# Linear attention with a gated MLP on one core: attention's last product in native fp32 with tokens on partitions, x normalized and turned before it leaves the chip, the fill finishing h with tanh, and blocks of 512 columns

## The chip, the core and the metric

The kernel runs on one core of a Trainium2 chip. Its engines work side by side and wait for each other by semaphores: TensorE (PE in the profile; PEld are its weight loads), VectorE (DVE), ScalarE (ACT), GpSimd (POOL), and SyncE (SP), which issues most DMAs. The metric is device time in microseconds from the first to the last instruction, lower is better.

## The reference, cut to what matters

```
phi(x):  proj = x @ w_phi;  proj -= max|proj|;  [exp(proj), exp(-proj)]      # 64 -> 2 x 128 features
kv  = phi(k)^T @ v          z = sum_s phi(k)                                  # per head
out = phi(q) @ kv / (phi(q) . z + 1e-6)                                       # B=8, H=8, S=576, D=64
x   = out, heads side by side: 4608 tokens x 512
xn  = x / sqrt(mean(x^2) + 1e-6) * rms_g
h   = silu(xn @ w_gate) * (xn @ w_val)                                        # 512 -> 1536, twice
result = h @ w_out                                                            # 1536 -> 512
```

All arrays are fp32.

## The kernel before, in words

Full precision is reached in two ways. A tile can be split into a rounded high part and a rest (`_split`, L59 to L61: a cast on ScalarE and a subtraction on VectorE or GpSimd), both in the type fp32r, and a product then takes three matmuls (high x high, high x low, low x high). Or a matmul takes fp32 operands as they are, which is called native fp32 below.

The work has three stages, all of it in one order that a scheduler of the framework makes from the program as written.

**Attention, with the first part of the MLP filled in.** 32 pairs of heads (8 batches x 4) run in a pipeline, one step of the loop at L500 per pair: `front` of pair i (transposes L298, projection in three fp32r matmuls L311 to L313, maximum L315, subtraction L318), `mid` of pair i-1, `back` of pair i-2, `last` of pair i-3. `mid` takes the exponentials of k (L338), makes kv with z as a 65th column in native fp32 (L351: 16 products of 128x128 with 128x65 per pair, two more with the remainder of 64 tokens, L346), splits kv into high and low (`kvs_`, L356), turns y of q so that features lie on partitions (L364), takes its exponential twice, in fp32 and rounded (L375, L376), and lets GpSimd subtract the two for the low half (L380). `back` multiplies with features as the contraction and kv as the stationary operand, 288 tokens at a time: 24 matmuls per pair (L415), evicted by ScalarE (L417) with the denominator in row 64. The denominator goes through DRAM to be spread over partitions, is inverted (L425), goes through DRAM again to be broadcast (L428), and `last` scales (L442, L443) and stores x by features (xs). A block of 288 columns that is complete in DRAM is fetched (`load_x`), split (`fill`, L465), and multiplied by the first three of the twelve column blocks of w_gate and w_val (`unit`, L474: 12 matmuls each); the products go to DRAM (gvs). rms_g has been multiplied into those weights.

Beside it the weights are decoded piece by piece (`decode_pieces`): one piece per step of the loop here, 24 pieces of w_out in the second stage.

**Gate and value.** 12 blocks of 384 columns, each with nine column blocks j: `gv` does 24 matmuls (L588) and silu times value (`hidden`, L571, L573), and h goes to DRAM (hs). `prep` (L145) fetches the next block of x, sums squares with a matmul against ones, normalizes and splits. `gv_raw` fetches the raw products of the fill, scales them with 1/rms and finishes them. The gate and value weights are loaded during the first block (`load_gv`, L561). The loop at L633 also pops the pieces of w_out, three a block from the second block on, and, once none are left, calls `load_o` (L608) at its steps 2 and 6 until four weight blocks of the output product are ready. `load_o` takes four DMAs into one of two buffers named wc, makes four differences in the other (L615) and splits both into wh and wl; its tiles lie in a pool of their own for the first four calls and in a pool that follows the gate and value weights in memory for the last two (L720).

**Output.** 18 groups of 256 tokens. `omm` (L737) does the seven products of Strassen's scheme, 18 matmuls of 256 columns each over the six weight blocks (L742); `operands` prepares the sums and splits of the next group.

Of the kernel before, what the change touches and what calls it, by code (L numbers as in the profile page):

```python
# [17 lines left out]

# [64 lines left out]
def kernel(ctx: ExitStack, tc: tile.TileContext, q, k, v, w_phi,  # L83
# [11 lines left out]
    SH = S // 2  # L95
    assert D == 64 and F == 128 and SR == 64 and T0 == 4 and NP == NC
    J1 = 3
    T = 384
    NB = N // T
    TF = S // 2  # L100
# [6 lines left out]
    gvs = dram.tile([J1 * 2 * 128, N], F32, name="gvs")  # L107
# [3 lines left out]
    wos = dram.tile([DF, DM], F32, name="wos")  # L111

    gl = ctx.enter_context(tc.tile_pool(name="gl", bufs=1))
    eps = gl.tile([128, 1], F32, name="eps")
    nc.vector.memset(eps, 1e-6)
    g = gl.tile([128, NC], F32, name="g")


# [4 lines left out]
    xm = x_ctx.enter_context(tc.tile_pool(name="xm", bufs=1))  # L123
    xops = [x_ctx.enter_context(tc.tile_pool(name="xo0", bufs=1))]
    xips = [x_ctx.enter_context(tc.tile_pool(name="xip", bufs=1))]
    xsv = xs.rearrange("(c p) n -> p c n", p=128)
    gvv = gvs.rearrange("(j w p) n -> j p w n", w=2, p=128)
    hsv = hs.rearrange("(j p) n -> p j n", p=128)

    one = gl.tile([128, 1], F32, name="one")  # L130
    nc.vector.memset(one, 1.0)
    epsd = gl.tile([128, 1], F32, name="epsd")
    nc.vector.memset(epsd, 0.0)
    nc.vector.memset(epsd[64:65], 1e-6)
    warm = gl.tile([128, 1], F32, name="warm")
    nc.scalar.activation(warm, one, AF.Exp)
    ones = gl.tile([128, 128], F32R, name="ones")
    nc.vector.tensor_copy(ones, one.broadcast_to([128, 128]))

    def fetch(bk, n=T, queue=None):  # L140
        x = xips[-1 if bk % 2 else 0].tile([128, NC * T], F32, name="x")[:, 0:NC * n].rearrange("p (c t) -> p c t", c=NC)
        (queue or nc.sync).dma_start(out=x, in_=xsv[:, :, bk * n:(bk + 1) * n])
        return x

    def prep(bk, x, pool, name):  # L145
        ss = xm.tile([128, T], F32, name="ss", bufs=1)
        nc.scalar.activation(ss, x[:, 0], AF.Square)
        for c in range(1, NC):
            sq = xm.tile([128, T], F32, name="sq", bufs=1)
            nc.scalar.activation(sq, x[:, c], AF.Square)  # L150
            nc.gpsimd.tensor_tensor(ss, ss, sq, ALU.add)  # L151
        sp = pool.tile([128, T], F32, name=name)
        sh = xm.tile([128, T], F32R, name="sq", bufs=1)
        sl = xm.tile([128, T], F32R, name="fo", bufs=3)
        _split(nc, sh, sl, ss, lo_eng=nc.gpsimd)
        nc.tensor.matmul(sp[:, 0:T], ones, sh, start=True, stop=False)
        nc.tensor.matmul(sp[:, 0:T], ones, sl, start=False, stop=True)
        ri = xm.tile([128, T], F32, name="ri", bufs=2)
        nc.scalar.activation(ri, sp[:, 0:T], AF.Sqrt, scale=1.0 / DM, bias=eps)
        nc.vector.reciprocal(ri, ri)  # L160
        for c in range(NC):
            nc.vector.scalar_tensor_tensor(x[:, c], x[:, c], g[:, c:c + 1], ri, ALU.mult, ALU.mult)
        xhl = xops[bk % len(xops)].tile([128, 2, NC, T], F32R, name="xb")
        _split(nc, xhl[:, 0], xhl[:, 1], x, lo_eng=nc.gpsimd)
        return xhl[:, 0], xhl[:, 1], ri
# [21 lines left out]

    a_ctx = ExitStack()
    xfp = a_ctx.enter_context(tc.tile_pool(name="a_xf", bufs=2))
    xips.append(a_ctx.enter_context(tc.tile_pool(name="a_xi", bufs=1)))  # L190
# [4 lines left out]
    big = a_ctx.enter_context(tc.tile_pool(name="a_big", bufs=2))  # L195
    dsc = a_ctx.enter_context(tc.tile_pool(name="a_dsc", bufs=3, space=DRAM))
# [6 lines left out]

# [9 lines left out]

    vms = [const.tile([128, 2, T0, D + 1], F32, name=f"vm{i}") for i in range(3)]
    vrs = [const.tile([128, 2, D + 1], F32, name=f"vr{i}") for i in range(3)]
# [5 lines left out]

    kvs = [[const.tile([128, 2, 2, 128], F32R, name=f"kv{i}{n}") for n in "hl"] for i in range(2)]
    for kp in kvs:
        for x in kp:
            nc.vector.tensor_copy(x[:, :, :, 64:128], w2[:, 2, 0:64].unsqueeze(1).unsqueeze(1).broadcast_to([128, 2, 2, 64]))

    def decode_jobs():
        jobs, late_ = [], []  # L230
        n = J1 * 128
        for wi, src in enumerate((w_gate, w_val)):
            for c in range(NC):
                def fill_w(w, wi=wi, c=c):
                    nc.vector.tensor_scalar(w, w, g[:, c:c + 1], None, ALU.mult)
                    _split(nc, wf1[wi][0][:, c], wf1[wi][1][:, c], w)
                jobs.append((src[c * 128:(c + 1) * 128, 0:n], n, fill_w))
# [29 lines left out]
    def load(pr):  # L267
# [14 lines left out]
        st[pr] = dict(kt=kt, qt=qt, rb=rb, hp=hp, b=b, vm=vm, vr=vr, kv=kvs[pr % 2])  # L282

    def front(pr):
# [7 lines left out]
        def trans(n):  # L294
            m = len(us[n]) * 128
            tp = ps_s.tile([128, 512], F32, name="sm")
            for j, u in enumerate(us[n]):
                nc.tensor.transpose(out=tp[:, j * 128:(j + 1) * 128], in_=u, identity=ident)  # L298
# [26 lines left out]
    def mid(pr):  # L325
        d = st[pr]
        y, vm, vr, (kh, kl) = d["y"], d["vm"], d["vr"], d["kv"]
        acc = ps_k.tile([128, 2, 2, D + 1], F32, name="acc")
        qh = big.tile([128, 2, 2, S], F32R, name="qh")
        ql = big.tile([128, 2, 2, S], F32R, name="ql")  # L330
        d.update(qh=qh, ql=ql)
# [12 lines left out]

# [9 lines left out]
        def kvs_():  # L354
            av = acc.rearrange("p a h d -> p h a d")
            _split(nc, kh[:, :, :, 0:D + 1], kl[:, :, :, 0:D + 1], av)  # L356


        def qexp(n, h):
            m = 4 if n == "q" else 1  # L360
            yp = ps_s.tile([128, 512], F32, name="sm")
            for j in range(m):
                src = y[n, h][:, j] if n == "q" else y[n, h][:, 1]
                nc.tensor.transpose(out=yp[:, j * 128:(j + 1) * 128], in_=src, identity=ident)  # L364
            if n == "q":
                hi, lo = qh[:, :, h, 0:SM], ql[:, :, h, 0:SM]
                eq = wk.tile([128, 2, 512], F32, name="eq")
                ei, yi = eq, yp
            else:
                hi, lo = qh[:, :, :, SM:S], ql[:, :, :, SM:S]  # L370
                eq = wk.tile([128, 2, 128], F32, name="eqr", bufs=1)
                ei = eq.rearrange("p a (h s) -> p a h s", h=2)
                yi = yp[:, 0:128].rearrange("p (h s) -> p h s", h=2)
            for sg in range(2):
                nc.scalar.activation(ei[:, sg], yi, AF.Exp, scale=1.0 - 2.0 * sg)  # L375
                nc.scalar.activation(hi[:, sg], yi, AF.Exp, scale=1.0 - 2.0 * sg)  # L376
                if n == "q":
                    for c in range(0, SM, SM // 2):
                        cs = slice(c, c + SM // 2)
                        nc.gpsimd.tensor_tensor(lo[:, sg, cs], ei[:, sg, cs], hi[:, sg, cs].bitcast(F32), ALU.subtract)  # L380
            if n != "q":
                nc.gpsimd.tensor_tensor(lo, ei, hi.bitcast(F32), ALU.subtract)
# [4 lines left out]
            lambda: qexp("q", 0),  # L387
# [3 lines left out]
            lambda: qexp("r", 0),  # L391
            lambda: qexp("q", 1),
# [3 lines left out]
            kvs_,  # L396
        ]


    def back(pr):  # L400
        d = st[pr]
        (kh, kl), qh, ql = d["kv"], d["qh"], d["ql"]
        nd = [big.tile([128, S], F32, name="nd", bufs=4) for _ in range(2)]
        dr = big.tile([128, S // 64], F32, name="dr", bufs=3)
        dd = dsc.tile([2, S], F32, name="dd")
        di = dsc.tile([2, S], F32, name="di")

        def num(h, c):
            cs = slice(c * SH, (c + 1) * SH)

            o = ps_f.tile([128, T], F32, name="fp") if pr < 12 else ps_s.tile([128, 512], F32, name="sm")
            i = 0
            for sg in range(2):
                for a, e in ((kh, qh), (kh, ql), (kl, qh)):
                    nc.tensor.matmul(o[:, 0:SH], a[:, h, sg], e[:, sg, h, cs], start=(i == 0), stop=(i == 5))  # L415
                    i += 1
            nc.scalar.activation(nd[h][0:D + 1, cs], o[0:D + 1, 0:SH], AF.Identity, bias=epsd[0:D + 1])  # L417
            if c == 1:
                nc.sync.dma_start(out=dd[h:h + 1], in_=nd[h][D:D + 1])
# [80 lines left out]
    for i in range(PR + 3):  # L500
# [18 lines left out]
        if len(units) <= 3:  # L519
            landed()  # L520
# [285 lines left out]
```

## Time and profile before

| | us |
|---|---|
| median of three runs | 1333.33 (1332.76 to 1334.62) |
| span of the profiled execution | 1337.6 |
| TensorE busy in it | 1288.5 |
| VectorE, ScalarE, GpSimd busy | 885.0, 711.0, 605.5 |
| first gate and value matmul (L588) starts | about 542 |
| first output matmul (L742) starts | about 1066 |

The profiled execution has no time of its own beside its span; the span lies 4.3 us above the median of the three runs. In the lines of the profile, `out<-in` are the program's tile names, `xN` the number of instructions, then come busy time, mean duration in ns, and the idle time before them with what ended it. Matmuls overlap, so the rate of TensorE is read from the distance of their starts. A native fp32 product has two records in the trace.

### The profile page before, as it was taken

The numbers are of one execution on the slowest core, as the hardware profiler recorded it, in microseconds if no ns is written. First come the engines' busy times: TensorE is split into PE (matmuls) and PEld (weight loads), VectorE is DVE, ScalarE is ACT, GpSimd is POOL, SyncE is SP. The second block draws the span as 40 slices with busy tenths as digits, with TensorE's granted clock in tenths as the row PEclk, the third lists the DMA queues.
The fourth block names the chain that finished last, engine by engine and source line by source line (L and its number), as shares of the span: only waits on it lengthen the run. The fifth ranks groups of instructions, "written<-read, shape, count | busy, mean of one in ns | idle before, by whom it ended". The sixth has DMA issues, their size and how long they took to land.

```text
span 1337.6 us, 25479 instructions
## 1 busy us (share of the span) xinstructions
PE 1288.5 (96%) x9396; PEld 1275.6 (95%) x9396; DVE 885.0 (66%) x1301; ACT 711.0 (53%) x1510; POOL 605.5 (45%) x568
## 2 busy tenths in 40 slices
PE   7989999999999896899999999999999999999998
PEld 7989899999999896899999999999999999999998
DVE  7899788778778773313456656655534498777784
ACT  5988877778778782434344344443333334434332
POOL 3766565555555570000233223233221078788684
PEclk9999999999999898999999999999999999999999
DMA  5555556566555434843454454554433534554451
GB/s 159 127 147 156 161 158 165 167 170 169 157 164 161 123 95 127 249 153 126 141 170 140 157 168 133 166 168 140 133 115 108 183 111 126 150 166 127 142 168 54
DMA packets 204524, 197.22 MB, mean 147 GB/s; under 512 B 69552, under 2 KB 186416, under 8 KB 204400
## 3 DMA queue, kind: packets, MB, share of 16 engines
q1 hardware_dynamic: 186448, 181.44, 45.2%
q10 hardware_dynamic: 17952, 14.16, 3.8%
q8 instruction: 74, 1.21, 0.4%
q14 instruction: 50, 0.41, 0.1%
HBM read 126.04 MB, written 69.50 MB: 146 GB/s over the span
## 4 chain that ended last, share of the span: by engine, by line
PE 57%; DMA 3%; DVE 1%; ACT 0%; issue 0%; POOL 0%; ACTq 0%; SPq 0%; DVEq 0%
PE fp L588 17%; PE gp L588 16%; PE gd L742 6%; PE gz L742 6%; PE gy L742 5%; PE fp L474 4%; PE fp L742 3%; DMA wc<-wvs 1%; DMA gvs<-fo 1%; DMA rc<-di 0%; PE sm L415 0%; DMA dd<-nd 0%; ACT fo L477 0%; POOL s2l L61 0%; DVE a12l L61 0%
## 5 line engine op out<-in xcount | busy, mean ns | idle before, releaser
L380 POOL TENSOR_TENSOR ql<-eq,qh 128x256 fp32r<-128x256 f32 x256 | 217.7, 882 | 67.3 <-issue 39.5
L588 PE MATMUL gp<-xb,wv 128*128 128x384 f32 x864 | 161.9, 334 | 0.8 <-ACT wv L60 0.8
L588 PE MATMUL fp<-xb,wg 128*128 128x384 f32 x864 | 161.0, 334 | 0.0
L573 DVE TENSOR_TENSOR h<-sl,gp 128x384 f32<-128x384 f32 x108 | 59.6, 552 | 144.2 <-PE gp L588 75.6
L588 PEld LDWEIGHTS gp<-xb,wv 128*128 128x128 f32 x864 | 150.7, 188 | 1.0 <-ACT wv L60 1.0
L571 ACT ACTIVATE sl<-fp 128x384 f32<-128x384 f32 x108 | 52.8, 489 | 185.6 <-PE fp L588 170.7
L588 PEld LDWEIGHTS fp<-xb,wg 128*128 128x128 f32 x864 | 150.7, 188 | 0.0
L54 POOL TENSOR_TENSOR wa<-raw,wa 128x192 f32<-128x192 f32 (+1 forms) x112 | 66.2, 613 | 162.2 <-issue 58.6
L351 PE MATMUL acc<-vm,ek 128*128 128x65 f32 x1024 | 131.8, 271 | 0.0
L315 DVE TENSOR_REDUCE mx<-pp 128x4 f32<-128x512 f32 (+1 forms) x160 | 100.6, 632 | 43.0 <-PE pp L313 41.5
L351 PEld LDWEIGHTS acc<-vm,ek 128*128 128x128 f32 x1024 | 128.1, 195 | 0.4 <-ACT ek L338 0.4
L151 POOL TENSOR_TENSOR ss<-ss,sq 128x384 f32<-128x384 f32 x36 | 37.6, 1044 | 160.6 <-ACT sq L150 160.6
L61 POOL TENSOR_TENSOR xb<-x,xb 128x1536 fp32r<-128x1536 f32 x12 | 42.5, 3540 | 132.3 <-ACT xb L60 124.6
L474 PE MATMUL fp<-xo,fg 128*128 128x288 f32 x576 | 92.8, 302 | 5.7 <-ACT fo L477 3.4
L376 ACT ACTIVATE qh<-sm 128x512 fp32r<-128x512 f32 (+1 forms) x192 | 97.3, 507 | 0.0
L474 PE MATMUL fp<-xo,fv 128*128 128x288 f32 x576 | 92.2, 300 | 4.4 <-ACT fo L477 4.4
L311 PE MATMUL pp<-wh,th 128*128 128x256 f32 x288 | 89.0, 310 | 2.7 <-DVE yr L318 2.1
L474 PEld LDWEIGHTS fp<-xo,fg 128*128 128x128 f32 x576 | 81.7, 190 | 7.4 <-ACT fo L477 4.4
L474 PEld LDWEIGHTS fp<-xo,fv 128*128 128x128 f32 x576 | 81.7, 190 | 5.1 <-ACT fo L477 5.1
L61 POOL TENSOR_TENSOR s2l<-st,s2h 128x768 fp32r<-128x768 f32 x18 | 43.5, 2419 | 95.0 <-ACT s2h L60 47.6
L375 ACT ACTIVATE eq<-sm 128x512 f32<-128x512 f32 x128 | 78.4, 612 | 14.1 <-PE sm L364 13.2
L313 PE MATMUL pp<-wh,tl 128*128 128x256 f32 x288 | 83.0, 298 | 1.8 <-DVE tl L61 1.8
(198 smaller groups left out, 3801.8 us busy)
## 6 DMA issues: line engine op xcount, KB each, us to landing
hs<-h SPq DMA_DIRECT2D x144, 192.0 KB
ht<-hs SPq DMA_DIRECT2D x18, 1536.0 KB
gvs<-fo SPq DMA_DIRECT2D x96, 144.0 KB
gvr<-gvs SPq DMA_DIRECT2D x36, 384.0 KB
rc<-di SPq DMA_DIRECT2D x32, 288.0 KB
x<-xs ACTq DMA_DIRECT2D x16, 576.0 KB
x<-xs SPq DMA_DIRECT2D x12, 768.0 KB
kt<-in_k_dram SPq DMA_DIRECT2D x32, 256.0 KB
```

The costliest lines, as they stand in the source:

```text
L54: nc.gpsimd.tensor_tensor(a[:, h], lf[:, h], a[:, h], ALU.mult)
L61: (lo_eng or nc.vector).tensor_tensor(lo, x, hi.bitcast(F32), ALU.subtract)
L311: nc.tensor.matmul(o, th[:, cs], wh, start=True, stop=False)
L313: nc.tensor.matmul(o, tl[:, cs], wh, start=False, stop=True)
L315: nc.vector.tensor_reduce(mx[:, 0:2 * m], pp[:, 0:2 * m], axis=AX.X, op=ALU.max, apply_absolute_value=True)
L351: nc.tensor.matmul(acc[:, sg, h], e[h][:, sg, j], vm[:, h, j], start=False, stop=(h == 1 and j == T0 - 1))
L375: nc.scalar.activation(ei[:, sg], yi, AF.Exp, scale=1.0 - 2.0 * sg)
L376: nc.scalar.activation(hi[:, sg], yi, AF.Exp, scale=1.0 - 2.0 * sg)
L380: nc.gpsimd.tensor_tensor(lo[:, sg, cs], ei[:, sg, cs], hi[:, sg, cs].bitcast(F32), ALU.subtract)
L474: nc.tensor.matmul(fp[:, 0:TF], w, xx[x][:, c], start=(i == 0), stop=(i == 3 * NC - 1))
L588: nc.tensor.matmul(gp[:, 0:T], w, e[:, c], start=(i == 0), stop=(i == 3 * NC - 1))
L742: nc.tensor.matmul(place[n], a[:, kp], w[:, o], start=(first and kp == 0 and i == 0), stop=(kp == KP - 1 and i == 2), skip_group_check=True)
```

## The change

- `mid` no longer splits kv (one copy instead, `kvt`) and takes each exponential of q once. `back` takes the exponentials as the stationary operand, 128 tokens at a time, and kvt as the moving one, 65 columns, in native fp32: for each head five token tiles (the fifth holds the remainders of both heads) times two signs. Tokens now lie on partitions, so the denominator is column 64 of the same tile; VectorE adds 1e-6, inverts and scales into x by tokens (`xt`, `xr`).
- Once the four pairs of a batch are done, `norm` squares and sums x on ScalarE, takes the power -1/2 on GpSimd, scales, turns x with 16 transposes on TensorE, multiplies by rms_g while copying, stores it and splits it for the fill, without a way back from DRAM. `norm_r` does the same for the 64 tokens that each head has over, two batches at a time. No division passes through DRAM, and `prep` and `gv_raw` are gone.
- A block is 512 tokens: eight blocks of one batch each and a ninth with the remainders. `unit` makes both products of a column block and finishes h by 0.5 (1 + tanh(g/2)) g v.
- The second stage begins with the remainders and the last batch, which are still on the chip, then fetches batches 0 to 6, already normalized. Its rules for the pieces of w_out and for `load_o` stand as they were, over nine blocks.

```
-    T = 384
+    T = SM
     NB = N // T
...
+        def kvs():
+            kvt = wk.tile([128, 2, 2, E1], F32, name="kvt")
+            nc.scalar.copy(kvt, acc)
+            d["kvt"] = kvt
...
             for sg in range(2):
-                nc.scalar.activation(ei[:, sg], yi, AF.Exp, scale=1.0 - 2.0 * sg)
-                nc.scalar.activation(hi[:, sg], yi, AF.Exp, scale=1.0 - 2.0 * sg)
...
+                nc.scalar.activation(eq[:, sg], yp, AF.Exp, scale=1.0 - 2.0 * sg)
...
+            for t in range(T0 + 1):
+                for sg in range(2):
+                    a = d["eq", h][:, sg, t * 128:(t + 1) * 128] if t < T0 else d["eq", "r"][:, sg]
+                    nc.tensor.matmul(o[:, t], a, kvt[:, sg, h], start=(t == 0 and sg == 0),
+                                     stop=(t == T0 and sg == 1), skip_group_check=True)
+            rc = wk.tile([128, T0 + 1], F32, name="rc")
+            nc.vector.tensor_scalar(rc, o[:, :, D], 1e-6, None, ALU.add)
+            nc.vector.reciprocal(rc, rc)
+            cs = slice((2 * hp + h) * D, (2 * hp + h + 1) * D)
+            nc.vector.tensor_tensor(xt[:, :, cs], o[:, 0:T0, 0:D],
+                                    rc[:, 0:T0].unsqueeze(2).broadcast_to([128, T0, D]), ALU.mult)
+            hr, br = (slice(i * 64, (i + 1) * 64) for i in (h, b % 2))
+            nc.vector.tensor_scalar(xr[br, cs], o[hr, T0, 0:D], rc[hr, T0:T0 + 1], None, ALU.mult)
...
+    def scaled(x, n):
+        ss = wk.tile([128, T0], F32, name="ss")
+        for t in range(n):
+            sq = wk.tile([128, DM], F32, name="sq", bufs=1)
+            nc.scalar.activation(sq, x[:, t], AF.Square, accum_out=ss[:, t:t + 1])
+        nc.vector.tensor_scalar(ss[:, 0:n], ss[:, 0:n], 1.0 / DM, 1e-6, ALU.mult, ALU.add)
+        nc.gpsimd.tensor_tensor(ss[:, 0:n], ss[:, 0:n], mhalf[:, 0:n], ALU.pow)
+        for t in range(n):
+            nc.vector.tensor_scalar(x[:, t], x[:, t], ss[:, t:t + 1], None, ALU.mult)
...
+        def turn(c):
+            tp = transposed([x[:, t, c * 128:(c + 1) * 128] for t in range(T0)])
+            nc.scalar.activation(xT[:, c], tp, AF.Copy, scale=g[:, c:c + 1])
+
+        def done():
+            nc.sync.dma_start(out=xsv[:, :, b * T:(b + 1) * T], in_=xT)
             with late():
...
+                filling.append((b, split_x(b, xT, nc.gpsimd)))
...
+            product(fp, [a[:, :, js] for a in wf1[wi]], x)
+            r.append(fp)
+            if wi == 0:
+                ft = xm.tile([128, T], F32, name="ft")
+                nc.scalar.activation(ft, fp, AF.Tanh, scale=0.5)
+                nc.vector.scalar_tensor_tensor(ft, ft, 1.0, fp, ALU.add, ALU.mult)
+        fh = xm.tile([128, T], F32, name="fh")
+        nc.vector.scalar_tensor_tensor(fh, ft, 0.5, r[1], ALU.mult, ALU.mult)
+        hidden(bk, j, fh)
...
+    order = [B, B - 1, *range(B - 1)]
...
-            if bk and n % (JN // J1) == 0 and decs:
+            if n and m % 3 == 0 and decs:
                 decs.pop(0)()
-            if not decs and len(wos_ops) < PRE and n % 4 == 2:
+            if not decs and len(wos_ops) < PRE and m % 4 == 2:
                 wos_ops.append(load_o(len(wos_ops), rg))
```

What stands on TensorE for a pair, in the middle of attention: before, the first head's `back` (`kv0h` and `kv0l` are the halves of kv, `qh` and `ql` those of the exponentials, `o` is in `sm`).

```order
L415 MATMUL sm<-qh,kv0h 128x288
L415 MATMUL sm<-ql,kv0h 128x288
L415 MATMUL sm<-qh,kv0l 128x288
L415 MATMUL sm<-qh,kv0h 128x288
L415 MATMUL sm<-ql,kv0h 128x288
L415 MATMUL sm<-qh,kv0l 128x288
L311 MATMUL pp<-wh,th 128x256
L312 MATMUL pp<-wl,th 128x256
```

Now, a head of a pair, and a turn of the batch before (`xt`):

```order
L347 MATMUL sm<-kvt,eq 128x65 x8
L347 MATMUL sm<-kvt,eqr 128x65 x2
L260 MATMUL pp<-wh,th 128x256
L261 MATMUL pp<-wl,th 128x256
L262 MATMUL pp<-wh,tl 128x256
L260 MATMUL pp<-wh,th 128x256
L261 MATMUL pp<-wl,th 128x256
L262 MATMUL pp<-wh,tl 128x256
L296 MATMUL acc<-vm_133,ek 128x65
L234 MATMUL sm<-ident,xt 128x128 x4
```

Twelve matmuls of 288 columns for a head (half of them shown) have become ten products of 65 columns, and four transposes have come in between.

What stands on ScalarE where the gate and value stage ends (`sl` is silu, `wh` a high half of output weights, `a11h` and the like the output's operands). Before, from the last two weight blocks on:

```order
L60 CAST wh_13279<-wc 128x768
L571 ACTIVATE sl<-fp 128x384
L571 ACTIVATE sl<-gvr 128x384
L60 CAST wh_13279<-wc 128x1024
L571 ACTIVATE sl<-fp 128x384 x3
L571 ACTIVATE sl<-gvr 128x384
L571 ACTIVATE sl<-fp 128x384 x3
L571 ACTIVATE sl<-gvr 128x384
L571 ACTIVATE sl<-fp 128x384
L60 CAST a11h<-ht 128x768
```

Now, from the last silu on:

```order
L512 ACTIVATE sl<-fp 128x512 x2
L51 CAST wh_10276<-wc 128x768
L51 CAST wh_10276<-wc 128x1024
L51 CAST a22h<-ht 128x768
L51 CAST a11h<-ht 128x768
L51 CAST a12h<-ht 128x768
L51 CAST s3h<-st 128x768
L51 CAST s1h<-ht 128x768
L51 CAST s2h<-st 128x768
L51 CAST wh_10292<-wc 128x768
L51 CAST wh_10292<-wc 128x1024
L51 CAST s4h<-st 128x768
```

The last weight block used to be cast nine silus ahead of the end; now the second of six is cast behind the last silu, and four more follow it, the third (`wh_10292`) among the operands and the other three behind them.

More of the change, by code (lines that the diff above doesn't have):

```diff
@@ L131 @@
[L131 to L165, printed above, removed]
+    xm = x_ctx.enter_context(tc.tile_pool(name="xm", bufs=2))
@@ L220 @@
         nc.gpsimd.memset(vr[0:64, 1], 0.0)
[L222 to L225, printed above, removed]
     def decode_jobs():
@@ L281, in load, with transposed @@
             nc.sync.dma_start(out=vr[hh * 64:(hh + 1) * 64, hh, 0:D], in_=v[b, h0 + hh, SM:S, :])
-        st[pr] = dict(kt=kt, qt=qt, rb=rb, hp=hp, b=b, vm=vm, vr=vr, kv=kvs[pr % 2])
+        st[pr] = dict(kt=kt, qt=qt, rb=rb, hp=hp, b=b, vm=vm, vr=vr)
+    def transposed(pieces):
+        tp = ps_s.tile([128, 512], F32, name="sm")
+        for j, u in enumerate(pieces):
+            nc.tensor.transpose(out=tp[:, j * 128:(j + 1) * 128], in_=u, identity=ident)
+        return tp
     def front(pr):
@@ L295, in trans @@
             m = len(us[n]) * 128
-            tp = ps_s.tile([128, 512], F32, name="sm")
-            for j, u in enumerate(us[n]):
-                nc.tensor.transpose(out=tp[:, j * 128:(j + 1) * 128], in_=u, identity=ident)
+            tp = transposed(us[n])
             th = wk.tile([128, 512], F32R, name="th")
@@ L395, in mid @@
             lambda: kv(1, 1),
-            kvs_,
+            kvs,
         ]
+    xts, xrs = {}, {}
+    xrt = xip.tile([128, NC, T], F32, name="xrt")
     def back(pr):
[L401 to L419, printed above, removed]
@@ L457 @@
[L457 to L479 removed]
+        d = st.pop(pr)
@@ new lines, with norm @@
+    filling, xb = [], {}
+    def norm(b):
+        x = xts.pop(b)
+        xT = xtp.tile([128, NC, T], F32, name="xT", bufs=1)
+        def turn(c):
[3 more added lines that the diff above has]
+            nc.sync.dma_start(out=xsv[:, :, b * T:(b + 1) * T], in_=xT)
+            with late():
+                filling.append((b, split_x(b, xT, nc.gpsimd)))
+        return [(0.0, lambda: scaled(x, T0))] + [(0.3 + 0.15 * c, lambda c=c: turn(c)) for c in range(NC)] + [(0.95, done)]
@@ new lines, in norm_r, with turn @@
+    def norm_r(b2):
+        x = xrs.pop(b2)
+        def turn():
+            tp = transposed([x[:, c * 128:(c + 1) * 128] for c in range(NC)])
+            nc.vector.tensor_tensor(xrt[:, :, b2 * 128:(b2 + 1) * 128], tp.rearrange("p (c n) -> p c n", c=NC),
+                                    g.unsqueeze(2).broadcast_to([128, NC, 128]), ALU.mult)
+            if b2 == B // 2 - 1:
+                nc.sync.dma_start(out=xsv[:, :, B * T:N], in_=xrt)
+                with late():
+                    filling.append((B, split_x(B, xrt, nc.gpsimd)))
+        return [(0.1, lambda: scaled(x.unsqueeze(1), 1)), (0.5, turn)]
@@ new lines, in hidden, with product, unit @@
+    def hidden(bk, j, h):
+        nc.sync.dma_start(out=hsv[:, j, bk * T:(bk + 1) * T], in_=h)
+    def product(o, w, x):
+        i = 0
+        for c in range(NC):
+            for a, e in ((w[0], x[0]), (w[0], x[1]), (w[1], x[0])):
+                nc.tensor.matmul(o, a[:, c], e[:, c], start=(i == 0), stop=(i == 3 * NC - 1))
+                i += 1
+    def unit(bk, x, j):
+        js = slice(j * 128, (j + 1) * 128)
+        r = []
+        for wi in range(2):
+            fp = ps_f.tile([128, T], F32, name="fp")
+            product(fp, [a[:, :, js] for a in wf1[wi]], x)
[7 more added lines that the diff above has]
+        hidden(bk, j, fh)
@@ L483 @@
     decs = decode_pieces(early, dec)
-    RES = 5 * J1 * 2
-    units, here = [], []
+    units = []
     dq = quota = 0.0
-    def load_x():
-        while fills and len(here) < 2:
-            bk = fills.pop(0)
-            here.append((bk, fetch(bk, TF, nc.scalar)))
+    RES = 9
     def landed():
-        if here:
-            units.extend(fill(*here.pop(0)))
+        while filling:
+            bk, x = filling.pop(0)
+            xb[bk] = x
+            units.extend(lambda j=j, bk=bk, x=x: unit(bk, x, j) for j in range(J1))
     load(0)
@@ L499 @@
     load(1)
-    for i in range(PR + 3):
+    total = NB * J1 - RES
+    for i in range(PR + 4):
         streams = []
```

259 lines of the change are left out of this document (89 added, 170 removed).

## The prediction

> **What bounds the kernel now.** I read the page's busy times first, then busy time by stage, then the chain of waits, and last the timeline of TensorE. The page:
>
> ```profile
> PE 1288.5 (96%) x9396; PEld 1275.6 (95%) x9396; DVE 885.0 (66%) x1301; ACT 711.0 (53%) x1510; POOL 605.5 (45%) x568
> ```
>
> TensorE (PE) is busy for 96% of the span. Where the other 4% lie, by stage (PE, PEld, DVE, ACT, POOL busy, then the granted clock):
>
> ```profile
> 0.00:200.00 200.00, 181.18 (x1448) 174.07 (x1449) 170.72 (x317) 159.31 (x392) 121.01 (x165) 1.00 0.57 151
> 200.00:430.00 230.00, 228.01 (x1888) 226.84 (x1887) 182.19 (x312) 177.15 (x443) 127.83 (x157) 1.00 0.60 167
> 430.00:500.00 70.00, 66.20 (x504) 65.38 (x504) 52.28 (x82) 56.29 (x135) 45.22 (x51) 0.93 0.36 101
> 500.00:620.00 120.00, 103.29 (x719) 100.42 (x718) 30.52 (x45) 45.28 (x100) 5.26 (x7) 0.96 0.55 169
> 620.00:1060.00 440.00, 440.00 (x2541) 440.00 (x2540) 239.11 (x365) 168.13 (x298) 104.57 (x100) 1.00 0.46 149
> 1060.00:1100.00 40.00, 37.14 (x295) 36.35 (x294) 34.62 (x26) 16.42 (x24) 25.70 (x11) 1.00 0.33 106
> 1100.00:1338.00 238.00, 232.72 (x2014) 232.51 (x2013) 175.54 (x157) 88.37 (x124) 175.92 (x80) 1.00 0.43 132
> ```
>
> Attention with the first fill units runs to about 500 us, the rest of the fill and the crossing into the gate and value products to 620, those products to 1066, then the output. TensorE idles 18.8 us in the first row, 2.0 and 3.8 in the next two, 16.7 at the crossing, 2.9 at the second crossing, 5.3 at the end, and the granted clock of 0.93 and 0.96 costs about another 5 us in each of its two rows. Everything else is work of TensorE, so the change is counted in matmuls first. What a matmul costs in a full stream is not its duration in a group but the distance to the next. From the chain (start, length, a run of matmuls):
>
> ```profile
> 697.49 2.08 PE fp L588 x12
> ...
> 1160.08 4.16 PE gy L742 x36
> ```
>
> A run of 12 matmuls of 384 columns takes 2.08 us of the chain: 173.3 ns each. 36 of 256 columns take 4.16 us: 115.6 ns. Both are 0.451 ns per column, with nothing fixed per matmul. From TensorE's timeline in attention:
>
> ```profile
> 349.41 0.29 PE L415 MATMUL sm<-qh,kv1h 128*128 128x288 f32 x1
> ...
> 351.00 0.28 PE L311 MATMUL pp<-wh,th 128*128 128x256 f32 x1
> ...
> 353.01 0.60 PE L364 MATMUL sm<-ident,yq 128*128 128x128 f32 x4
> 353.36 0.36 PE L311 MATMUL pp<-wh,th 128*128 128x256 f32 x1
> 353.56 0.28 PE L312 MATMUL pp<-wl,th 128*128 128x256 f32 x1
> ...
> 357.01 1.67 PE L351 MATMUL acc<-vm,ek 128*128 128x65 f32 x14
> 358.49 0.38 PE L415 MATMUL sm<-qh,kv0h 128*128 128x288 f32 x1
> 358.71 0.29 PE L415 MATMUL sm<-ql,kv0h 128*128 128x288 f32 x1
> ```
>
> Twelve matmuls of L415 fill 349.41 to 351.00: 132.5 ns each. Four transposes take 0.35 us, and the matmul behind them 0.20 instead of 0.12: 0.43 us, 108 ns each. L351 is the one product that is native fp32 today, a 128x128 stationary operand against 65 moving columns:
>
> ```profile
> L351 PE MATMUL acc<-vm,ek 128*128 128x65 f32 x1024 | 131.8, 271 | 0.0
> ```
>
> The kernel issues 512 of them (16 for each of 32 pairs) and the trace has 1024 records, two for each. The 14 records above are seven products; they take 1.48 us and lengthen the next matmul by 0.09: 1.57 us, 224 ns a product.
>
> **The change part by part, on TensorE.** (1) The last product of attention. Out go 24 L415 matmuls a pair, 768 in all: 768 x 0.1325 = -101.8 us. In come 20 native fp32 products a pair (two heads, five token tiles, two signs), 640 in all, each the very form of L351: 640 x 0.224 = +143.4 us. Net +41.6. Fewer instructions, but each pays for a fresh stationary operand and uses it for 65 columns only. (2) x turned on TensorE: 16 transposes for each of 8 batches and 4 for each of 4 pairs of batches, 144 x 0.108 = +15.6 us. (3) The 24 matmuls against ones that summed squares: 24 x 0.173 = -4.2 us. (4) Blocks of 512 columns: the same columns in fewer matmuls. At 0.451 ns per column the gate and value products cost the same (2592 x 173.3 = 1944 x 231.1 = 449.2 us); the fill goes from 1152 x 132.5 = 152.6 to 648 x 231.1 = 149.8, -2.8 us. Sum of TensorE's work: +50.2 us.
>
> The title FP8 and Floating Point Precision of the Trainium skill (TensorE Precision Notes) says that true fp32 is four passes through the array. Columns alone would then make a product 4 x 65 x 0.451 = 117 ns, and the sum 68 us smaller; the L351 row says 224, and its 512 products are the same shape, so the sum goes by the row. TensorE: Matmul & The Clock Gate (Weight-path perf modes) has a reason that fits the row: its fast weight load is not used for fp32.
>
> **Waits that go.** In the first 200 us TensorE waits (waiting instruction, releaser, us in total, times, longest):
>
> ```profile
> PE sm L298 <- POOL vr L218: 3.7, 1, 3.7
> PE sm L298 <- DMA rb<-in_q_dram: 2.6, 1, 2.6
> PE pp L311 <- DVE yr L318: 2.1, 1, 2.1
> PE fp L415 <- ACT kv1h L60: 1.7, 2, 1.2
> PE sm L298 <- DVE tl L61: 1.6, 3, 0.7
> PE fp L415 <- DVE kv1l L61: 1.4, 2, 1.2
> ```
>
> The first two (6.3 us) are the start and stay; the kv split goes, and the rest is VectorE and ScalarE being late. Per pair ScalarE loses six exponentials (the hi half) and four evictions, GpSimd the whole ql subtraction, VectorE the DMA-bound division. What VectorE keeps is heavy, what it gains is small:
>
> ```profile
> L315 DVE TENSOR_REDUCE mx<-pp 128x4 f32<-128x512 f32 (+1 forms) x160 | 100.6, 632 | 43.0 <-PE pp L313 41.5
> ```
>
> ```profile
> 507.27 0.22 DVE L425 RECIPROCAL dr<-dr 128x9 f32<-128x9 f32 x1 [3.21 <-DMA dr<-dd]
> ```
>
> It adds eight operations a pair (add, reciprocal, two scalings for each head), by the 0.22 us of such a narrow one and about 0.4 for the 256-column one some 2 us a pair, and sheds about as much (L442, L443, the reciprocal, the kv split). TensorE's own work grows by 1.3 us a pair (41.6 / 32), so its partners have more room. I let 12 of the 18.8 us go, bounds 0 and 12.5 (all but the start). In 200 to 500 the stalls stem from the block prepared by L518 and from VectorE being held by splits of x; the split of x goes to GpSimd: 8 of the 10.7 us (idle and clock) go, bounds 0 and 10.
>
> At the first crossing TensorE waits for copies of fill results that wait for their stores, and for the division's trips through DRAM:
>
> ```profile
> PE fp L474 <- ACT fo L477: 7.7, 7, 2.0
> ```
>
> Both go. The new chain stays on chip: behind the last product four squares on ScalarE, a power on GpSimd, four scalings, 16 transposes, four copies, casts and low halves.
>
> ```profile
> L150 ACT ACTIVATE sq<-x 128x384 f32<-128x384 f32 x36 | 18.7, 520 | 12.9 <-POOL ss L151 12.5
> ```
>
> ```profile
> L61 POOL TENSOR_TENSOR xb<-x,xb 128x1536 fp32r<-128x1536 f32 x12 | 42.5, 3540 | 132.3 <-ACT xb L60 124.6
> ```
>
> At 0.6 us a ScalarE pass and 2.4 us for a GpSimd half block it is about 20 us long; the fill matmuls that stand behind the last product cover 10 of them (44 x 0.231), transposes 2. So 8 us stay idle and about 4 are lost to the clock that falls after such a gap (the rows 430:500 and 500:620, the two with gaps, are the ones with 0.93 and 0.96). 21.8 becomes 12.5: -9 us, bounds -18 and +5.
>
> **A wait that comes.** The output weights (load_o, six pairs of row blocks) are made ready during the gate and value stage, from w_out as the decode pieces finish it. There are 24 such pieces, three per block from the second block on. With 12 blocks they end in the ninth; the load_o follow in the blocks behind it, and the last one is done at 1039.8 in the trace, 26 us before the stage ends. With 9 blocks they end in the last one at its seventh step, where one load_o follows; the other five go to the pool that takes over the memory of the gate and value weights, and their casts stand behind the last silu on ScalarE. What one costs, from the tile wc in the last of them today:
>
> ```profile
> L60 ACT CAST wh<-wc x4: 827/938/1050, 1027.6 to 1037.2; 128x768 fp32r<-128x768 f32 x2, 128x1024 fp32r<-128x1024 f32 x2
> L61 DVE TENSOR_TENSOR wl<-wc,wh x4: 951/1087/1221, 1030.9 to 1038.6; 128x768 fp32r<-128x768 f32 x2, 128x1024 fp32r<-128x1024 f32 x2
> L614 SPq DMA_DIRECT2D wc<-wos x4: 319/424/430, 1031.9 to 1033.2; - x4
> L615 DVE TENSOR_TENSOR wc<-wc x4: 418/425/426, 1034.7 to 1036.4; 128x256 f32<-128x256 f32 x4
> ```
>
> From the first DMA at 1031.9 to the end of the second low half at 1039.8 is 7.9 us, and the two wc buffers let the next one start only when this one's first low half is done: about 6 us each in a row. VectorE also makes the first operands then, and beside GpSimd its operations stretch:
>
> ```profile
> 1067.25 0.95 DVE L61 TENSOR_TENSOR a11l<-ht,a11h 128x768 fp32r<-128x768 f32 x1
> 1068.12 2.61 DVE L61 TENSOR_TENSOR a12l<-ht,a12h 128x768 fp32r<-128x768 f32 x1
> ```
>
> The same operation takes 0.95 and 2.61 us. Followed step by step, VectorE first works through the second and third weight block and the operands (about 20 us, half of it stretched), then the last three blocks' first low halves stand at 25, 31 and 37 us: the last one 37 us after the last gate and value matmul. Before it TensorE can do four of the seven products of one group for five weight blocks (60 matmuls, 6.9 us); 66 follow (7.6 us). The first group ends at 45 us instead of 14.6: 30 us of wait and about 2 for the clock, against the 2.9 of today. +30 us, bounds +2 (if the five loads are early after all) and +42 (7.9 us each, in a row, with stretched splits).
>
> **The sum.** 1337.6 + 50.2 - 12 - 8 - 9 + 30 = 1388.8 us for a profiled execution. The span of the profile is 4.3 us above the median of 1333.33, so I forecast 1384.5, rounded to 1384.
>
> **The rivals.** *The output weights are hidden.* The scheduler hoists their loads and the wait is that of today: 1384 - 28 = 1356 us. For it: the first load_o does stand early on VectorE. Against: the second one's casts stand behind the last silu, in memory that is still in use. Chance 0.19. *VectorE becomes the bound of attention.* If a narrow operation on PSUM takes 1 us instead of 0.3, eight of them make 5 us a pair more; VectorE, now at 0.85 of the first 200 us, then holds up the eight pairs that run before any fill, and the 12 and 8 us above do not go: about 1404. Chance 0.14. *The native product costs its columns only:* each of its two records passes twice over 65 columns, 117 ns a product, and the load of the stationary operand hides behind the product before it: 640 x 0.107 = 68 us less, 1316 us, faster. It decides from below 0.144 us a product, with the other terms as they are: 51 us are to be had back out of 640 products, 0.080 each. Only L351's row speaks on it, against: in no run does it come near that. Chance 0.05, of which 0.01 lies near no change.
>
> **How the numbers follow.** The forecast has 0.62. The range 1356 to 1404 takes in the hidden weights at its lower end and the VectorE case at its upper end and leaves out the cheap product and the outermost sums. A measurement of this kernel can tell 0.2%, 2.7 us, from no change. Faster 0.04, same 0.01, slower 0.95.
>
> **What would show it.** In the profile after: 1280 records of the new product, a run of 20 of them 2.24 us long; fill matmuls 231 ns apart; the gate and value stage again 449 us without a gap; in attention VectorE and ScalarE well under TensorE; at the second crossing about 30 us of idle TensorE with the clock down, ended by low halves of the output weights. I am wrong on the main term if a run of ten products takes clearly less than 2.2 us, and on the second if TensorE's idle time at that crossing stays under 10 us.

## The result, and the profile after

| | before | after |
|---|---|---|
| median of four runs, us | 1333.05 (1327.86 to 1334.62) | 1365.76 (1363.20 to 1366.65) |
| span of the profiled execution | 1337.6 | 1364.9 |

The ratio is 1.0247, 95% interval 1.0225 to 1.0268: 2.5% slower. The spans differ by 27.3 us.

The page of after, engines:

```profile
PE 1329.1 (97%) x8876; PEld 1218.4 (89%) x8876; DVE 753.5 (55%) x1329; ACT 531.9 (39%) x1054; POOL 350.0 (26%) x264
```

Fewer matmuls keep TensorE busy for longer, while every partner has lost work: VectorE 131.5 us, ScalarE 179, GpSimd 255.5. By stage (the columns of the prediction's table; the second crossing lies at 1055 to 1105 now):

```profile
0.00:200.00 200.00, 191.31 (x1567) 186.08 (x1567) 151.23 (x339) 115.67 (x267) 30.01 (x49) 1.00 0.41 115
200.00:430.00 230.00, 230.00 (x1822) 219.82 (x1821) 161.59 (x353) 122.95 (x283) 33.07 (x36) 1.00 0.39 112
430.00:500.00 70.00, 70.00 (x554) 66.79 (x553) 48.78 (x111) 38.68 (x90) 11.01 (x12) 1.00 0.37 108
500.00:620.00 120.00, 116.80 (x740) 104.27 (x740) 67.13 (x130) 53.27 (x110) 21.19 (x15) 0.97 0.31 103
620.00:1055.00 435.00, 435.00 (x1921) 360.32 (x1920) 96.31 (x192) 82.79 (x149) 54.68 (x62) 1.00 0.27 95
1055.00:1105.00 50.00, 31.15 (x142) 26.45 (x141) 36.89 (x41) 19.27 (x24) 15.52 (x7) 0.62 0.24 81
```

Up to 620 us TensorE now idles 8.7 + 0 + 0 + 3.2 = 11.9 us instead of 41.3, and between 200 and 500 us not at all. Nearly all of the 8.7 is the start, as the row from 20 us on shows:

```profile
20.00:200.00 180.00, 179.40 (x1508) 174.78 (x1507) 142.56 (x320) 106.90 (x249) 26.56 (x31) 1.00 0.39 110
```

The row of the second crossing shows the new hole: 18.9 us idle in 50 and a granted clock of 0.62. The new product, on TensorE's timeline:

```profile
301.56 0.60 PE L234 MATMUL sm<-ident,xt 128*128 128x128 f32 x4
301.99 0.56 PE L296 MATMUL acc<-vm,ek 128*128 128x65 f32 x4
302.39 1.95 PE L347 MATMUL sm<-kvt,eq 128*128 128x65 f32 x16
304.17 0.61 PE L347 MATMUL sm<-kvt,eqr 128*128 128x65 f32 x4
304.62 0.28 PE L234 MATMUL sm<-ident,yr 128*128 128x128 f32 x1
```

Ten products are 20 records and take 2.23 us, 223 ns each. Four transposes of x take 0.43 us, 108 ns each. The chain gives the long matmuls:

```profile
783.69 2.72 PE gp L408 x12
...
1126.60 4.28 PE gz L649 x36
```

Twelve matmuls of 512 columns take 2.72 us (226.7 ns each, 0.443 per column, not 0.451). In the output 36 of 256 columns take 4.28 us, 118.9 ns each, where before had 4.16 us and 115.6, with the same code. At the second crossing TensorE waits most for:

```profile
PE fp L649 <- DVE a11l L52: 5.6, 1, 5.6
PE fp L649 <- ACT wh L51: 5.2, 2, 2.7
PE fp L649 <- ACT a11h L51: 3.3, 1, 3.3
PE fp L649 <- DVE wl L52: 1.6, 4, 0.8
```

and the chain through it goes over the last weight blocks:

```profile
1055.69 2.73 PE gp L408 x12
...
1084.33 2.77 DMA wc<-wos
...
1090.55 2.43 DMA wc<-wos
...
1094.22 0.88 DVE wl L52
1095.15 0.80 PE fp L649 x2
...
1105.18 2.16 PE fp L649 x18
```

The first low halves of the last three weight blocks end at 1083.0, 1089.2 and 1095.1, which is 25, 31 and 37 us behind the last gate and value matmul (1058.4), and the second group of the output begins at 1105.2. From 1070 to 1100 us the granted clock is 0.50, and two matmuls in a row stand 0.21 us apart instead of 0.12.

### The profile page after: what moved, and what is told of

It reads as the page before. It is cut to its first block, busy times and chain, and to the rows that moved or that the text cites. A ratio compares the mean times of both kernels' runs of the same rounds, so it can differ in the third digit from the quotient of the medians.

```text
span 1364.9 us, 22642 instructions
## 1 busy us (share of the span) xinstructions
PE 1329.1 (97%) x8876; PEld 1218.4 (89%) x8876; DVE 753.5 (55%) x1329; ACT 531.9 (39%) x1054; POOL 350.0 (26%) x264
## 4 chain that ended last, share of the span: by engine, by line
PE 54%; DVE 2%; DMA 1%; ACT 0%; SPq 0%; issue 0%; ACTq 0%; DVEq 0%
PE fp L408 19%; PE gp L408 16%; PE gy L649 6%; PE gz L649 6%; PE gd L649 6%; PE fp L649 3%; DMA wc<-wos 1%; DVE wc L526 0%; DVE wl L52 0%; SPq L525 0%; ACT xb L51 0%; DVE st L589 0%; DVE a11l L52 0%; DVE a12l L52 0%; DVE st L586 0%
## 5 line engine op out<-in xcount | busy, mean ns | idle before, releaser
L408 PE MATMUL fp<-xb,fg 128*128 128x512 f32 x648 | 164.0, 397 | 1.4 <-ACT xb L51 1.4
L408 PE MATMUL gp<-xb,wv 128*128 128x512 f32 x648 | 156.6, 390 | 1.2 <-ACT xb L51 1.2
L408 PE MATMUL fp<-xb,wg 128*128 128x512 f32 x648 | 155.3, 389 | 0.0
L408 PEld LDWEIGHTS fp<-xb,fg 128*128 128x128 f32 x648 | 120.4, 189 | 25.7 <-ACT xb L51 1.7
L347 PE MATMUL sm<-kvt,eq 128*128 128x65 f32 x1024 | 121.6, 272 | 0.0
L347 PEld LDWEIGHTS sm<-kvt,eq 128*128 128x128 f32 x1024 | 119.9, 192 | 0.2
L408 PE MATMUL fp<-xb,fv 128*128 128x512 f32 x324 | 86.0, 401 | 0.0
L284 ACT ACTIVATE ek<-yk 128x512 f32<-128x512 f32 x128 | 75.9, 632 | 16.1 <-PE acc L296 11.4
L261 PE MATMUL pp<-wl,th 128*128 128x256 f32 x288 | 81.9, 284 | 0.0
L408 PE MATMUL gp<-xb,fv 128*128 128x512 f32 x324 | 77.8, 389 | 0.0
```

The costliest lines, as they stand in the source:

```text
L261: nc.tensor.matmul(o, th[:, cs], wl, start=False, stop=False)
L284: nc.scalar.activation(e[h][:, sg], y["k", h], AF.Exp, scale=1.0 - 2.0 * sg)
L347: nc.tensor.matmul(o[:, t], a, kvt[:, sg, h], start=(t == 0 and sg == 0), stop=(t == T0 and sg == 1), skip_group_check=True)
L408: nc.tensor.matmul(o, a[:, c], e[:, c], start=(i == 0), stop=(i == 3 * NC - 1))
```

## The experiments

The theory in short: TensorE sets the time nearly everywhere; the native products cost 224 ns each and make the kernel slower; the relieved partners give back the waits; late output weights cost some 28 us at the second crossing. Each run was timed beside the kernel before on the same chip, and ratios are to it (1335.41 us in the first four, 1335.99 in the next three, 1333.88 in the last two). Where a run is set against the kernel after, that is a difference of ratios, 1.0247 for after, good to about 4 us.

**Output weights earlier.**

```
-            if n and m % 3 == 0 and decs:
+            if n and m % 2 == 0 and decs:
```

> The kernel after, with the pieces of w_out popped at every second step of a block of the second stage instead of every third (five a block instead of three), so that the four load_o that the loop may call come before its end; nothing else is changed. Theory (the output weights are late, and their casts and low halves are what TensorE waits for at the second crossing): the wait of about 31 us falls to about the 4 us of the kernel before, and the time to 1365.8 - 27 = 1339 us, between 1335 and 1345. Rival (what counts there is the first operands, a11h and a11l, which TensorE waited 8.9 us for, and a clock that falls in any gap; the weights are only behind them): at most 9 us go, 1357 to 1366 us.

Measured: 1345.19 us, ratio 1.0068 (1.0046 to 1.0090), 24 us less than after. Busy time from 1040 to 1110 us, of after and of this run:

```profile
1040.00:1110.00 70.00, 51.15 (x250) 43.88 (x249) 45.26 (x52) 24.23 (x34) 21.41 (x11) 0.73 0.23 75
```

```profile
1040.00:1110.00 70.00, 64.73 (x429) 59.73 (x428) 48.79 (x42) 23.89 (x34) 31.22 (x14) 0.93 0.25 79
```

In the same 70 us TensorE does 429 matmuls instead of 250, at a clock of 0.93 instead of 0.73. So most of the hole was the weights, and the rival is out as the main cause. It was not wholly wrong: of the 8.9 us that TensorE waited for the first operands, 4.8 stay.

```profile
PE fp L649 <- ACT a11h L51: 2.6, 1, 2.6
PE fp L649 <- DVE a11l L52: 2.2, 1, 2.2
```

**The product twice, and half of it.** Each run of ten issued twice:

```
+            for rep in range(2):
                 for t in range(T0 + 1):
                     for sg in range(2):
```

> The kernel after, with each run of ten native products issued twice into the same sums (numerator and denominator both double, the quotient stays): 640 more products. Theory (a product takes 224 ns of TensorE whatever stands beside it, and TensorE alone sets the time of attention): +143 us, 1509 us, between 1502 and 1514. Rival one (a product costs its columns only, 117 ns, and the rest of the 224 is a wait that the run before it hides): +75 us, 1441 us. Rival two (other engines hold attention, and TensorE has room): clearly less than +143, by the idle time that TensorE then fills.

Measured: 1508.02 us, ratio 1.1285 (1.1266 to 1.1304), 139 us more than after; the spans differ by 141.6, 221 ns a product. Then only the positive exponential (`a = d["eq", h][:, 0, ...]`, no loop over sg):

> The kernel after with only the products of the positive exponential: ten a pair instead of twenty, 320 fewer (the output leaves out the half of the features with the negative sign). Theory (the waits of attention went because ScalarE, GpSimd and the trips through DRAM were relieved, so that TensorE stays the bound even with less to do): -72 us, 1294 us, between 1289 and 1298. Rival (they went because TensorE became slower and its partners got more time per pair; with 2.2 us a pair less the partners hold it up again): some 10 to 20 us of waits come back in the first 500 us, 1304 to 1314 us.

Measured: 1296.91 us, ratio 0.9708 (0.9687 to 0.9728), 72 us less than after, 225 ns for each of the 320 products left out. Its first two stages:

```profile
0.00:200.00 200.00, 190.64 (x1519) 183.36 (x1520) 164.15 (x375) 130.84 (x303) 33.18 (x54) 1.00 0.46 130
200.00:430.00 230.00, 230.00 (x1791) 218.17 (x1790) 180.68 (x408) 143.40 (x324) 39.69 (x41) 1.00 0.44 125
```

TensorE stays as full as in after although a pair has 2.2 us less for it. The price holds in both directions, and the waits did not go because TensorE became slower: its partners have room.

**The remainder tile once for both heads.**

```
+            for t in range(T0 + h):
...
+                    if t < T0:
+                        p, a, w = o[:, t], d["eq", h][:, sg, t * 128:(t + 1) * 128], kvt[:, sg, h]
+                    else:
+                        p, a, w = o[:, T0:m].rearrange("p t e -> p (t e)"), d["eq", "r"][:, sg], kvt[:, sg].rearrange("p h e -> p (h e)")
```

> The kernel after, with the remainder tile of a pair multiplied once for both heads (per sign one product with 130 moving columns instead of two with 65): 18 products a pair instead of 20, the same columns in all. Theory (a native product of this form has a fixed price of 224 ns, and 130 columns cost no more than 65): 64 x 0.224 = -14.3 us, 1351.5 us, between 1349 and 1355. Rival (the price goes by columns): no change, 1364 to 1367 us.

Measured: 1353.36 us, ratio 1.0124 (1.0104 to 1.0144), 16 us less than after. 64 products fewer at the same number of columns: the price is for the product, not for its columns.

**One pass in fp32r.** `kvt`, `eq` and `eqr` as fp32r, E1 = D + 2:

> The kernel after, with the exponentials of q and kv rounded to fp32r for the last product, and 66 columns instead of 65: the same 640 products with the same stationary tiles, in one pass (the output leaves out the low halves of both). Theory (the 224 ns are passes, each with its own load of the stationary tile, so one pass costs a quarter of the four): 56 ns, 640 x 0.168 = -107 us, about 1261 on a chip where the kernel after takes 1368. Rival one (two records of 112 ns; a fresh stationary tile costs about the 108 ns of a transpose whatever the type): -74 us, about 1294. Rival two (the stationary load is not overlapped at all for 66 columns and is as long as for native fp32): no change to -20 us.

Measured: 1298.59 us, ratio 0.9717 (0.9687 to 0.9747), 71 us less than after, 111 ns saved a product. Its timeline:

```profile
237.49 0.98 PE L347 MATMUL sm<-kvt,eq 128*128 128x66 f32 x8
238.29 0.39 PE L347 MATMUL sm<-kvt,eqr 128*128 128x66 f32 x2
238.52 0.33 PE L234 MATMUL sm<-ident,yr 128*128 128x128 f32 x1
```

Ten products are now ten records in 1.03 us, and by the total each has become cheaper by half of its price: rival one. My theory of four passes with a load each fell. What costs some 111 ns is a record with a fresh stationary tile of 128 columns and few moving columns, in fp32r as in native fp32; the native product has two such records. Only the first record of a run behind a long matmul is different, and there the passes show. In this run it stands 33 ns ahead of the second, and the other nine take 111 each (0.03 + 9 x 0.111 = 1.03 us). The first record of a run of native products stands 56 to 58 ns ahead of the second (medians over the runs in before and in after). At 0.451 ns a column that is 66 columns once (30 ns) and 65 columns twice (59 ns), so a native record does seem to pass twice over its columns. Inside a run that does not show: every further record of either type takes 111 to 112 ns. Three fp32r products in place of a native one, to keep full precision, would by that cost about 330 ns against 224 (an estimate, not run).

**Before, with one exponential.** L375 and the subtractions at L380 and L382 out, and

```
-                for a, e in ((kh, qh), (kh, ql), (kl, qh)):
+                for a, e in ((kh, qh), (kh, qh), (kl, qh)):
```

> The kernel before, with each exponential of q taken once (rounded) and no low half: ScalarE loses six passes a pair and GpSimd its subtractions, as in the change; TensorE keeps its 24 matmuls, the middle ones with the high half in place of the low (the output leaves out the low half of the exponentials of q). Theory (the waits of TensorE in the first 500 us came from ScalarE and GpSimd, and this relief alone takes most of them away): of the 24.6 us of idle time there 12 to 18 go, and with the clock some 12 to 20 us of the time, 1315 to 1323 beside 1335. Rival (they came from what else the change took out: the division's trips through DRAM, the way of the raw products, VectorE's splits of x): less than 5 us go, 1330 to 1336.

Measured: 1322.92 us, ratio 0.9893 (0.9856 to 0.9930), 14 us less than before, inside the expected range. But the waits went elsewhere than I expected:

```profile
0.00:200.00 200.00, 180.42 (x1402) 177.16 (x1403) 152.63 (x306) 126.78 (x307) 19.42 (x44) 0.95 0.58 148
200.00:430.00 230.00, 230.00 (x1921) 230.00 (x1920) 172.90 (x324) 154.84 (x366) 20.11 (x30) 1.00 0.61 169
430.00:500.00 70.00, 69.61 (x568) 69.18 (x567) 48.23 (x87) 48.39 (x112) 13.41 (x13) 1.00 0.45 130
500.00:620.00 120.00, 112.01 (x763) 109.51 (x762) 33.63 (x49) 49.76 (x103) 4.06 (x4) 0.97 0.56 174
```

Of the 24.6 us of idle time in the first 500 us only 4.6 went, where the expectation had 12 to 18; at the first crossing, where I had expected nothing, it fell from 16.7 to 8.0. From 200 to 500 us it is nearly gone (0.4 us). In the first 200 it is 19.6 us at a clock of 0.95, against 18.8 at 1.00 before, and most of it has another name (TensorE's waits there; then what ended the idle time ahead of ScalarE's evictions into nd between 80 and 200 us, in us and times):

```profile
PE fp L408 <- ACT nd L410: 7.6, 6, 2.7
```

```profile
DMA xs<-nd: 7.4, 3
```

Three evictions, 7.4 us in all, stood until a store of x had left nd. That was tested next, in the same kernel without ql:

```
-        nd = [big.tile([128, S], F32, name="nd", bufs=4) for _ in range(2)]
+        nd = [big.tile([128, S], F32, name="nd", bufs=8) for _ in range(2)]
```

> The kernel before with one exponential of q and no low half, as above, and with eight buffers instead of four for the evicted products nd, in the memory that the low half leaves free. In the run above TensorE still waited in the first 200 us, for evictions that stood until a store of x had left their buffer. Theory (the division's trips through DRAM and the stores of x hold nd, and that made the other half of the early waits): the waits of 20 to 200 us fall from about 22 us lost to under 5, and the time by 15 to 20 us, to 1303 to 1308 beside 1323. Rival (the queues of the DMAs are late by themselves, or VectorE and ScalarE are short of time there; more buffers only put the wait off): less than 5 us, 1318 to 1323.

Measured: 1309.27 us, ratio 0.9814 (0.9783 to 0.9845), about 11 us less than the run above; the expectation had 15 to 20.

```profile
0.00:200.00 200.00, 186.61 (x1541) 184.65 (x1542) 166.16 (x334) 140.83 (x333) 21.98 (x48) 0.98 0.61 160
```

Idle time there falls from 19.6 to 13.4 us, the clock rises from 0.95 to 0.98, and the matmuls rise from 1402 to 1541.

Idle time alone doesn't add up to these times, so here is lost time: a stretch less what the matmuls begun in it cost at full rate (112 ns a native record, 108.5 a transpose, 118.5, 132.5, 173.3 and 226.7 for 256, 288, 384 and 512 columns, the distances of their starts in full stretches). Stretches of after without idle time come out at -1.5 to 0 us, so it is good to about 2 us.

| lost time in us | before | one exponential | with eight buffers | after |
|---|---|---|---|---|
| 0 to 20 | 12.4 | 13.2 | 12.0 | 13.0 |
| 20 to 100 | 9.3 | 0.8 | 0.6 | 0.1 |
| 100 to 200 | 8.1 | 21.3 | 6.0 | -0.4 |
| 200 to 500 | 11.5 | -0.8 | 4.3 | -1.5 |
| 500 to 620 | 23.4 | 13.7 | 13.3 | 6.6 |
| sum | 64.8 | 48.1 | 36.2 | 17.7 |

The exponentials with their low halves made the waits of 20 to 100 us. With them gone a second cause came out between 100 and 200: evictions without a free nd, which the way of the quotient through DRAM holds. More buffers took 15 us of that away, but 5 came back behind 200 us, so the rival (they only put the wait off) was right for a third. Eight buffers beside the full exponentials were not run. The change takes out both causes; the 18 us between the last two columns are what else it took out, and no run splits them.

**Both edits, and 32 bytes.** Early weights and remainder once, together:

> The kernel after with two edits together: the pieces of w_out at every second step, and the remainder tile multiplied once for both heads. Alone they took 24 and 16 us off. Theory (different stages, both on TensorE's path): they add up, -40 us, 1328 us where the kernel before takes 1335, that is 0.5% below it. Rival (one takes cover from the other): 1335 us or more.

Measured: 1330.35 us, ratio 0.9961 (0.9944 to 0.9978): they add up. The same with a tile of 16 bytes, in a 32-byte place, ahead of all others (`shift = gl.tile([128, T0], F32, name="shift")`):

> The kernel of the two edits (early weights, remainder once) with one more small tile ahead of all others, so that weights and operands start 32 bytes later in memory, as they stand in the kernel before; the instructions are the same. Theory (where the operands start decides the rate of the long fp32r matmuls, and that is why the output's, whose code nothing changed, run at 118.9 ns here and at 115.6 in the kernel before): a run of 36 of them takes 4.16 us instead of 4.27, and a run of 12 matmuls of 512 columns 2.77 instead of 2.72, at 0.451 ns a column; -7 and +11 us, 1332 to 1336. Rival (the rate hangs on the order of the work or on the width of the blocks): both runs stay, 1330 us.

Measured: 1324.35 us, ratio 0.9934 (0.9913 to 0.9955), the best version here, 0.7% below before. The chains of the two kernels, first without the shift, then with it:

```profile
579.76 2.72 PE fp L414 x12
...
1105.96 4.27 PE gz L655 x36
```

```profile
579.69 2.72 PE fp L416 x12
...
1075.70 4.16 PE gz L657 x36
```

The output has before's 115.6 ns again, 63 runs of 36 by 0.11 us, 6.9 us in all; the spans differ by 6.3. The matmuls of 512 columns stay at 226.7 ns (12 in 2.72 us), so there my theory was wrong. The intervals of the two ratios overlap; it is the rows that show the effect. The two runs were on different chips, but the rate does not go by the chip: the kernel before with one exponential, on the chip of the first, has 115.6 ns there too, and with eight buffers, on the chip of the second, the same. A kernel of the change without the shift was not run on the second chip.

## Why the prediction was right and wrong

Slower, and for the reasons given. The forecast of 1384 us lies 18 above the result, as much as one term is off: the waits of the first 620 us, which I had at -29, came out at -47, and the other misses nearly cancel. The time alone could not have shown the second reason: 1365.76 lies nearer to the 1356 of the rival whose output weights are hidden than to 1384. It is the rows of the second crossing and the first run that show it. Step by step, on the spans:

- **TensorE's work, +50.2: right in its main terms.** 223 ns a product against 224 from L351, 108 ns a transpose against 108; the product twice and halved confirm it in the total. Two small terms were missed: 512 columns do not cost 0.451 ns each (2592 matmuls, 4.4 ns cheaper: -11.4 us), and the output, which I left unchanged, has 2268 matmuls 3.3 ns dearer (+7.5 us). Sum about +46; that the two nearly cancel is luck.
- **The reason named for the price: open.** That fast weight load is not used for fp32 (the Trainium skill, TensorE: Matmul & The Clock Gate, Weight-path perf modes) was not tested: an fp32r record of this shape costs the same 111 ns, so the price of a record is not special to native fp32, but whether a fast load would lower it no run here shows. The four passes of true fp32 (the Trainium skill, FP8 and Floating Point Precision, TensorE Precision Notes) fit the first record of a run (two records of two passes), but they do not set the price: native fp32 has two records and twice the price of one. The section LDWEIGHTS of TensorE: Matmul & The Clock Gate in the Trainium skill gives a load as its columns divided by 1.2, which makes an estimate of 107 ns for 128 columns, and the rows agree: 108 for a transpose, 111 to 112 for a record of either type. The number came from the row and stood.
- **Waits of the first 200 us, -12: too small, and the cause named only in part.** Idle time 18.8 became 8.7, -10.1, but the lost time fell from 29.8 to 12.7, -17, beyond my bound of 12.5. I credited the partners' relief alone; in the run with one exponential it clears 20 to 100 us, but the first 200 as a whole lose 35.3, because the evictions then wait for nd.
- **200 to 500 us, -8: too small.** All of it went: 5.8 us idle and 4.9 of clock (0.93 in a row of 70), -10.7, over my bound of 10; by lost time -13. I had named VectorE's splits of x; with these as they were, the run with one exponential takes 12 of it away.
- **First crossing, -9: too small.** 21.5 us of idle time and clock became 3.2 + 3.6, -14.7; by lost time 23.4 became 6.6, -17. The run with one exponential takes 10 of it, with the stores and the division's trips through DRAM, which I had named, still in place. I had the on-chip chain 20 us long and covered for 12; TensorE waits there only for one copy of xT and two casts of x:

```profile
PE fp L408 <- ACT xb L51: 1.4, 1, 1.4
...
PE gp L408 <- ACT xb L51: 1.2, 1, 1.2
PE sm L234 <- ACT xT L378: 0.6, 1, 0.6
```

- **What idle time and clock leave out.** By them these three come to -35.5 beside the forecast -29; the lost time says -47, and with that the spans close: 46 - 47 + 28 (below) = 27. I had priced a stall at its idle time. In the kernel before:

```profile
501.65 0.29 PE L415 MATMUL sm<-ql,kv1h 128*128 128x288 f32 x1
507.82 0.61 PE L415 MATMUL sm<-qh,kv1l 128*128 128x288 f32 x1 [5.88 <-DVE kv1l L61]
508.23 0.44 PE L415 MATMUL sm<-qh,kv1h 128*128 128x288 f32 x1
508.47 0.44 PE L415 MATMUL sm<-ql,kv1h 128*128 128x288 f32 x1
```

Between the first two starts lie 6.17 us, 6.04 more than the 0.13 of such a matmul, beside 5.88 of idle time: a record is 0.29 us long but the next may start after 0.13, and idle time is counted from the record's end. The next ones stand 0.41 and 0.24 apart, so a stretch at about half rate follows. The clock column does not go with idle time either: the first row of before has the most (18.8 us) and a clock of 1.00, so my remark that the rows with gaps are those with the lower clock leaves that row out.

- **Second crossing, +30: right, in place, mechanism and size.** The last three low halves came 25, 31 and 37 us behind the last gate and value matmul, as forecast, and the first group ended at 47 us against 45. The lost time of this row, from its 142 matmuls (15 of 512 columns, 127 of 256, 18.5 us at full rate), is 31.5 us; before's row of 40 us, with 37 of 384 columns and 258 of 256 (36.2 us), lost 3.8. That is +28, of which the first run gave 24 back. Only the split was off: not 30 us of idle time and 2 for the clock but 19 of idle time, the rest matmuls at a clock of 0.50. And of the waits named, the first operands (8.9 us) come before the weights (5.2 and 1.6): they stood behind the weights' casts and low halves, for with early weights 4.8 are left.
- **From span to median, -4.3: wrong.** After has its span 0.9 us below its median. The offset of one kernel's profiled execution is not the other's. That is why the medians differ by 32.7 us and the spans by 27.3. In nearly all timed executions on record the span is 1.7 to 2.1 us below the time, so before's profiled one, with 1337.6, was likely some 6 us slower than its median, and some 6 of the 47 us of waits may be that execution's own.

Rivals: hidden weights are refuted by the crossing's rows and the first run. VectorE as the bound is refuted by the row of 20 to 200 us, where TensorE idles 0.6 us; its new operations take 0.16 to 0.42 us each, 2.1 us a pair, as estimated. The price by columns is refuted by three runs (the product twice, half of it, the remainder once).

## What to carry over

In a run of matmuls with few moving columns each record costs about 111 ns, most likely the load of its stationary tile, and native fp32 has two records a product: count fresh stationary tiles, not columns, and let one tile serve more columns where it can (130 for the price of 65 here). When blocks become fewer, look at every rule that counts steps per block; one digit in such a rule was worth 24 us. A stall costs more than the gap that the profile shows, so count what its stretch got done; and behind the cause of a wait that you take away a second one may stand.

## What was not expected of the hardware

The start of the tiles in memory changes the rate of the output's fp32r matmuls with 256 moving columns: 118.6 ns in the one kernel, 115.6 in the other, where nearly all tiles start 32 bytes further on and nothing else differs but one small memset on VectorE. Which of the operands matters stays open, and only this one shift was tried. With 512 columns no such change was seen (2.72 us for 12 in both places), and a column there costs 0.443 ns where 384 columns cost 0.451.
